# Streaming weight slices in pairs: eight transfers of 768 KB and three buffers in place of fifteen of 384 KB and five

## The chip, the cores and the metric

The kernel runs on one core of a Trainium2 chip. The metric is device time of one execution in microseconds (us). The engines are TensorE (PE, with its weight loads shown as PEld), VectorE (DVE), ScalarE (ACT), GpSimd (POOL) and SyncE (SP, which only issues transfers here).

## The reference

Two attention layers over the same input are mixed by a gate. `A` is recurrent: 64 segments of 32 tokens, and 8 memory rows that each segment hands to the next. All 32 heads of 192 use the same weights in every segment.

```
for s in range(64):                                   # x: [1, 2048, 640], segments of 32
    h = concat([mem, x[:, 32*s:32*s+32]], axis=1)     # 8 + 32 rows of 640
    q, k, v = h @ Wq, h @ Wk, h @ Wv                  # each [640, 32 heads, 192]
    p = softmax(where(mask, q @ k.T * 192**-0.5, -1e9))
    o = (p @ v) @ Wo                                  # [32, 192, 640]
    mem, out_a[s] = o[:, :8], o[:, 8:]
b = sliding_dilated_attention(x, wqkv, wo)            # window 8, dilation 2, 32 heads of 20
g = sigmoid((x * gate_w).sum(-1))
out = g * out_a + (1 - g) * b                         # bf16 in and out
```

## The kernel before

The program has four stages. `part_b` computes layer B and the gate. `prepass` projects the last 8 tokens of every segment ahead of time, into `zpk_dram`. `part_a` is the loop over the 64 segments, the main loop. `part_z` finishes the rows that were left for the end.

The weights Wq, Wk, Wv and Wo are cut into 80 slices of [128, 1536] bf16, 384 KB each: five slices (`kc` 0 to 4) for each of four column blocks `R` of q, k and v, twelve slices `oa` and eight `ob` of Wo. They do not all fit on chip. 65 of them stay resident (tiles `wres_*` and `wlate_*`), and 15 are streamed from DRAM again in every segment through a pool `wstream` of `WBUFS` = 5 buffers, tile name `wst`. `weights_setup` picks the streamed ones: it lays all 80 on an estimated time line of one segment and takes the slice nearest to each of 15 evenly spaced points. They are, in the order of use: q(0,2), k(0,4), q(1,4), q(2,0), k(2,0), q(3,0), k(3,0), v(0,0), v(1,1), v(2,0), v(3,0), oa 0, oa 5, oa 7 and ob 4. The four of Wo are first rewritten into a DRAM scratch `wscr` so that each partition's row is contiguous.

In a segment PE runs, in the order that `part_a` writes down: q and k of the four blocks (`m_qk`, line 540), their transposes (`t_qk`, 554), scores (`s_a` and `s_b`, 577 and 586), v (`m_v`, 623), the softmax sums (`e_norm`), p times v (`pv_half`, 643 and 647), and the output projection (`o_group`, 680). The last part of that order is

```
m_v(2); pv_half(0); e_norm(1); m_v(3)
for i2 in range(6): o_group("oa", i2)
pv_half(1)
for i2 in range(3): o_group("ob", i2)
for i2 in range(6, 12): o_group("oa", i2)
load_z(s + 1)
for i2 in range(3, 12): o_group("ob", i2)
```

so `oa` 0 to 5 come before `pv_half(1)`, and `ob` 0 and 1 come right behind it, before `oa` 6 to 11. The memory rows of the next segment come out of `sel` (line 690) by way of two copies on ACT into `whi` (lines 746 and 754; the profile calls this tile ZQ, of which it is a part). `load_z` (lines 513 and 514) is issued on ACT's queue between these two copies, and brings 96 KB into `KZ` and 96 KB into `ZQ`; the first scores of the next segment read that part of `ZQ`.

The streamed slices are loaded by SP, one transfer for each (`load_slice`, lines 381 and 383). SP issues in program order, and each issue waits until the buffer is free, that is until PE has finished with the slice that came five streamed slices earlier. Each transfer writes 128 rows of 3072 bytes.

Of the kernel before, what the change touches and what calls it, by code (L numbers as in the profile page):

```python
# [10 lines left out]
BF = mybir.dt.bfloat16  # L11
F32 = mybir.dt.float32
I32 = mybir.dt.int32

N_STREAM = 15
N_LATE = 55
N_LATE2 = 22
WBUFS = 5

_DEV = {"mode": "full"}  # L20

# [3 lines left out]
class _K:  # L25
# [313 lines left out]
    def weights_setup(self):  # L339
        nc, tc = self.nc, self.tc  # L340
        keys = self.slice_keys()
        gap = {("q", 0, 3): 200, ("k", 0, 3): 0, ("q", 1, 0): 620, ("k", 1, 0): 270, ("q", 2, 0): 570, ("k", 2, 0): 270,
               ("q", 3, 0): 980, ("k", 3, 0): 270, ("v", 0, 0): 690, ("v", 1, 0): 270, ("v", 2, 0): 710,
               ("v", 3, 0): 1160, ("oa", 6): 1530, ("q", 0, 0): 200}
        at, t = {}, 0
        for k in keys:
            t += gap.get(k, 0)
            at[k] = t
            t += 163
        self.stream_keys = set()  # L350
        for i in range(N_STREAM):
            left = [k for k in keys if k not in self.stream_keys]
            self.stream_keys.add(min(left, key=lambda k: abs(at[k] - (i + 0.5) * t / N_STREAM)))
        rest = [k for k in keys if k not in self.stream_keys]
        first = ["q", "k", "v", "oa", "ob"]
        self.late = sorted(rest, key=lambda k: first.index(k[0]))[-N_LATE:]
        self.wres = self.ctx.enter_context(tc.tile_pool(name="wres", bufs=1))
        self.res_tiles = {}
        self.wscr = {}
        self.early = [k for k in rest if k not in self.late]  # L360
        self.wstream = self.ctx.enter_context(tc.tile_pool(name="wstream", bufs=WBUFS))

    def load_early(self):

        for k in self.early:
            self.res_tiles[k] = self.load_slice(self.wres, k, "wres_" + "_".join(map(str, k)))
        so = sorted(k for k in self.stream_keys if k[0] in ("oa", "ob"))
        scr = self.dram.tile([len(so), 128, 1536], BF, name="wscr")
        for i, k in enumerate(so):
            src, split = self.slice_info(k)  # L370
            self.nc.sync.dma_start(scr[i].rearrange("p (c f) -> p c f", c=split[0]), src)
            self.wscr[k] = scr[i]

    def load_slice(self, pool, key, name, tag=None, t=None):
        src, split = self.slice_info(key)
        kw = {"tag": tag} if tag else {}
        if t is None:
            t = pool.tile([128, 1536], BF, name=name, **kw)
        v = t if split is None else t.rearrange("p (c f) -> p c f", c=split[0])
        if key in self.wscr:  # L380
            self.nc.sync.dma_start(t[:], self.wscr[key])
        else:
            self.nc.sync.dma_start(v[:], src)
        return v

    def load_late(self, part):

        pool = self.ctx.enter_context(self.tc.tile_pool(name=f"wlate{part}", bufs=1, reuse_waits="tile"))
        ks = (self.late[:-N_LATE2], self.late[-N_LATE2:-1], self.late[-1:])[part]
        first = ks[:4] if part == 1 else []  # L390
        place = [k for k in ks if k not in first] + first
        tiles = {k: pool.tile([128, 1536], BF, name="wlate_" + "_".join(map(str, k))) for k in place}
        for k in ks:
            self.res_tiles[k] = self.load_slice(None, k, None, t=tiles[k])

    def get_slice(self, key):
        if key in self.res_tiles:
            return self.res_tiles[key]
        return self.load_slice(self.wstream, key, "wst", "wst")

    def prepass(self):

# [484 lines left out]
```

## Time and profile before

| | |
|---|---|
| median of 3 runs | 1902.32 us (1899.49 to 1911.51) |
| the profiled execution | 1907.39 us, its span 1905.7 us |
| granted TensorE clock, mean over the span | 0.985 |
| `part_b` and the first part of `prepass` | PE begins `ps_pre` (line 425) at 229 us |
| main loop | 411 to 1849 us, 64 segments |
| `part_z` | from 1849 us |
| PE busy in the span | 1729.0 us (91%) |
| DMA, mean of the 16 engines, 800 to 1000 us | busy 0.91, 296 GB/s |
| HBM read over the span | 446.61 MB |

A time in the profile counts from the start of the span. The busy share of PE is that of pipelined matmuls. The DMA share is the mean over 16 engines of the time that their packets took. Queue q1 carries what SP issues, q10 what ACT issues, and q8 the instruction blocks that the engines fetch.

### The profile page before, as it was taken

The page shows a single profiled execution, that of the slowest core. Times are in us where ns is not written, and L with a number is a line of the kernel's source. Part 1 is how long each engine was busy: PE and PEld are TensorE (multiplying, and loading weights), DVE is VectorE, ACT ScalarE, POOL GpSimd, SP SyncE. Part 2 cuts the span into 40 slices and gives each one's busy share as a digit, 9 for nine tenths or more (in the row PEclk, how much of TensorE's full clock was granted, in tenths as well). Part 3 has the DMA queues.
Part 4 walks back from the last instruction along what each step waited for, and adds up shares of the span by engine and source line. Part 5 has one row for each costly group of instructions (what it writes and reads, how often), then busy time and mean ns, then how long its engine had stood idle before and what let it go on. Part 6 is the DMA issues. An engine that isn't in the chain of part 4 may idle for free.

```text
span 1905.7 us, 91340 instructions
## 1 busy us (share of the span) xinstructions
PE 1729.0 (91%) x41120; PEld 1022.0 (54%) x41135; DVE 655.9 (34%) x2047; ACT 743.4 (39%) x1865; POOL 69.5 (4%) x135
## 2 busy tenths in 40 slices
PE   6998999779999999999999899989999999999989
PEld 3554544335555555555555555555555555555557
DVE  4565433223333333333333333333333333333330
ACT  3776522123333343333333333333443333333340
POOL 4010000010000000000000000000000000000000
PEclk9999999989999999999999999999999999999999
DMA  6510395979889899899989888989999898998991
GB/s 176 177 44 16 100 308 137 303 203 291 282 287 297 283 296 292 287 301 292 303 291 296 284 278 290 295 281 287 297 299 293 289 293 284 295 289 282 294 295 31
DMA packets 299434, 486.88 MB, mean 255 GB/s; under 512 B 99236, under 2 KB 168356, under 8 KB 299044
## 3 DMA queue, kind: packets, MB, share of 16 engines
q1 hardware_dynamic: 182680, 420.92, 67.7%
q10 hardware_dynamic: 116364, 60.12, 11.3%
q8 instruction: 322, 5.28, 1.1%
q14 instruction: 68, 0.56, 0.1%
HBM read 446.61 MB, written 35.91 MB: 253 GB/s over the span
## 4 chain that ended last, share of the span: by engine, by line
PE 73%; DMA 9%; ACT 7%; issue 5%; DVE 3%; ACTq 2%; SPq 0%; DVEq 0%
PE ps_qk L540 22%; PE ps_v L623 12%; PE ps_wo L680 10%; PE ps_qkT L554 6%; PE ps_pre L425 5%; DMA ZQ<-zpk_dram 4%; PE ps_S L577 3%; PE ps_bqk L220 3%; PE ps_z L819 3%; PE ps_oT L643 3%; ACT bP L243 2%; DMA zpk_dram<-ZV 2%; DMA wst<-in_A_Wk_dram 2%; ACT KV L545 1%; DVE KV L653 1%
## 5 line engine op out<-in xcount | busy, mean ns | idle before, releaser
L545 ACT CAST KV<-ps_qk 128x384 bf16<-128x384 f32 x512 | 239.4, 480 | 415.0 <-PE ps_qk L540 411.4
L540 PEld LDWEIGHTS <-hT 128*32 128x32 bf16 x10240 | 237.6, 96 | 192.2 <-issue 75.1
L540 PE MATMUL ps_qk<-wlate_k,hT 128*32 128x384 bf16 x4352 | 248.4, 328 | 11.0 <-ACT ZQ L754 6.6
L623 PE MATMUL ps_v<-wlate_v,hT 128*32 128x384 bf16 x4096 | 228.0, 329 | 6.0 <-issue 5.8
L680 PEld LDWEIGHTS <-KV 128*32 128x32 bf16 x6144 | 172.4, 98 | 111.0 <-DVE KV L653 33.6
L540 PE MATMUL ps_qk<-wres_q,hT 128*32 128x384 bf16 x2560 | 164.8, 331 | 28.5 <-ACT KV L545 15.9
L557 DVE COPY ZQ<-ps_qkT 128x384 bf16<-128x384 bf16 x256 | 91.2, 356 | 250.6 <-PE ps_qkT L554 250.2
L680 PE MATMUL ps_wo<-wlate_oa,KV 128*32 128x384 bf16 x2304 | 160.3, 339 | 12.8 <-issue 4.0
L540 PE MATMUL ps_qk<-wst,hT 128*32 128x384 bf16 x1792 | 154.5, 331 | 1.7 <-issue 1.5
L623 PEld LDWEIGHTS <-hT 128*32 128x32 bf16 x5120 | 113.8, 96 | 70.7 <-issue 12.9
L554 PE MATMUL ps_qkT<-ident,KV 128*128 128x128 bf16 x1536 | 141.2, 221 | 3.8 <-DVE ZQ L616 1.7
L653 DVE CAST KV<-ps_oT 128x192 bf16<-128x192 f32 x256 | 79.9, 353 | 186.4 <-ACT KV L653 186.4
L680 PE MATMUL ps_wo<-wlate_ob,KV 128*32 128x256 bf16 x2688 | 134.9, 280 | 10.2 <-issue 10.2
L554 PEld LDWEIGHTS <-KV 128*128 128x128 bf16 x1536 | 87.6, 97 | 95.0 <-issue 93.7
L680 PE MATMUL ps_wo<-wst,KV 128*32 128x384 bf16 (+1 forms) x1152 | 124.1, 319 | 5.4 <-issue 3.5
L653 ACT CAST KV<-ps_oT 128x192 bf16<-128x192 f32 x256 | 69.8, 325 | 123.7 <-PE ps_oT L647 122.2
L540 PE MATMUL ps_qk<-wlate_q,hT 128*32 128x384 bf16 x1536 | 108.3, 330 | 0.0
L577 PE MATMUL ps_S<-ZQ,KV 128*32 128x40 bf16 (+1 forms) x4096 | 99.6, 186 | 8.3 <-DMA ZQ<-zpk_dram 6.8
L577 PEld LDWEIGHTS <-KV 128*32 128x32 bf16 (+1 forms) x4096 | 77.7, 92 | 47.4 <-issue 10.8
L693 DVE CAST hT<-ps_mem 128x24 bf16<-128x24 f32 x126 | 22.6, 179 | 214.6 <-PE ps_mem L690 214.6
L627 ACT CAST KV<-ps_v 128x384 bf16<-128x384 f32 x128 | 61.4, 479 | 84.1 <-DMA a<-bsc_dram 50.7
L623 PE MATMUL ps_v<-wst,hT 128*32 128x384 bf16 x1024 | 89.1, 336 | 1.2 <-issue 1.2
(130 smaller groups left out, 2214.4 us busy)
## 6 DMA issues: line engine op xcount, KB each, us to landing
wst<-in_A_Wq_dram SPq DMA_DIRECT2D x260, 384.0 KB
wst<-in_A_Wv_dram SPq DMA_DIRECT2D x260, 384.0 KB
wst<-wscr SPq DMA_DIRECT2D x256, 384.0 KB
wst<-in_A_Wk_dram SPq DMA_DIRECT2D x195, 384.0 KB
zpk_dram<-ZS ACTq DMA_DIRECT2D x4, 3072.0 KB
ZQ<-zpk_dram ACTq DMA_DIRECT2D x128, 96.0 KB
wlate_k<-in_A_Wk_dram SPq DMA_DIRECT2D x17, 384.0 KB
wlate_v<-in_A_Wv_dram SPq DMA_DIRECT2D x16, 384.0 KB
```

Of the source, the lines that this page charges most:

```text
L220: nc.tensor.matmul(ps[:, 0:nn], lhsT=wqk[n][:, kc, 4 * g:4 * g + 4, :].rearrange("p h d -> p (h d)"), rhs=xT[:, kc, o0:o0 + nn], start=(kc ...
L425: nc.tensor.matmul(ps[:], lhsT=sls[kc][:, c0:c0 + 128], rhs=zT[:, kc, :], start=(kc == 0), stop=(kc == KC - 1))
L540: nc.tensor.matmul(pq[32 * j:32 * j + 32, 0:384], lhsT=hT[:, kc, :], rhs=sl[:, 384 * j:384 * j + 384], start=(kc == 0), stop=(kc == KC - 1 ...
L545: nc.scalar.copy(st, pq[:, 0:384])
L554: nc.tensor.transpose(pT[:, t, :, :, :].rearrange("p j b i -> p (j b i)"), st[:, 128 * t:128 * t + 128], self.ident[:])
L557: nc.vector.tensor_copy(q_blocks(R)[:, 1:5, :, :].rearrange("p b c i -> p c b i"), pT.rearrange("p t j b i -> p (t j) b i"))
L577: nc.tensor.matmul(pSs[h][32 * j:32 * j + 32, par, 40 * r:40 * r + 40], lhsT=KT[k0:k1, 12 * r + c, :], rhs=q_blocks(R)[k0:k1, :, c, :], st ...
L623: nc.tensor.matmul(pv[32 * j:32 * j + 32, 0:384], lhsT=hT[:, kc, :], rhs=sl[:, 384 * j:384 * j + 384], start=(kc == 0), stop=(kc == KC - 1 ...
L627: nc.scalar.copy(V[R], pv[:, 0:384])
L643: nc.tensor.matmul(out[:, r, t, :], lhsT=V[2 * h + r][ks, f0:f1], rhs=E[ks, par, 40 * r:40 * r + 40], start=(r == 0 and t == 0), stop=Fals ...
L653: cp(oTxs[2 * h + j // 2][:, 6 * (j % 2):6 * (j % 2) + 6, :], pos[j // 2][:, j % 2, 0:240].rearrange("p (c q) -> p c q", q=40)[:, :, 8:40])
L680: nc.tensor.matmul(pso[part][32 * jj:32 * jj + 32, 0:n], lhsT=oTxs[2 * (R // 2) + j // 2][:, 6 * (j % 2) + 3 * (R % 2) + t, :], rhs=o_weig ...
```

## The change

Streamed slices are chosen, loaded and freed in neighbouring pairs. `N_STREAM` goes from 15 to 16 and `WBUFS` from 5 to 3, with buffers of twice the size. 64 slices stay resident instead of 65. The pairs, in order of use, are k(0,0-1), k(1,0-1), k(2,2-3), k(3,0-1), v(1,0-1), v(2,2-3), oa 4-5 and ob 0-1. One transfer writes 256 runs of 3072 bytes (q, k, v) or 128 runs of 6144 bytes (from `wscr`). A pair's transfer is issued where its first slice is asked for, and its buffer is free when PE has finished with the second.

```diff
-N_STREAM = 15
+N_STREAM = 16
-WBUFS = 5
+WBUFS = 3
...
-        for i in range(N_STREAM):
-            left = [k for k in keys if k not in self.stream_keys]
-            self.stream_keys.add(min(left, key=lambda k: abs(at[k] - (i + 0.5) * t / N_STREAM)))
+        pairs = [(k, k[:-1] + (k[-1] + 1,)) for k in keys
+                 if k[-1] % 2 == 0 and not (k[0] in "qkv" and k[-1] == self.KC - 1)]
+        self.pairs, self.held, self.stream_keys = {}, {}, set()
+        for i in range(N_STREAM // 2):
+            left = [p for p in pairs if p[0] not in self.stream_keys]
+            p = min(left, key=lambda p: abs((at[p[0]] + at[p[1]]) / 2 - (i + 0.5) * t / (N_STREAM // 2)))
+            self.stream_keys.update(p)
+            self.pairs.update({k: p for k in p})
...
-        scr = self.dram.tile([len(so), 128, 1536], BF, name="wscr")
+        scr = self.dram.tile([128, len(so), 1536], BF, name="wscr")
...
+    def load_pair(self, first):
+
+        src, split = self.slice_info(first)
+        t = self.wstream.tile([128, 2, 1536], BF, name="wst", tag="wst")
+        if first in self.wscr:
+            self.nc.sync.dma_start(t[:], self.wscr[first])
+            return [t[:, i, :].rearrange("p (c f) -> p c f", c=split[0]) for i in range(2)]
+        W = {"q": self.Wq, "k": self.Wk, "v": self.Wv}[first[0]].rearrange("(c p) f -> p c f", p=128)
+        self.nc.sync.dma_start(t[:], W[:, first[2]:first[2] + 2, first[1] * 1536:(first[1] + 1) * 1536])
+        return [t[:, i, :] for i in range(2)]
...
     def get_slice(self, key):
         if key in self.res_tiles:
             return self.res_tiles[key]
-        return self.load_slice(self.wstream, key, "wst", "wst")
+        p = self.pairs[key]
+        if key == p[0]:
+            self.held.update(zip(p, self.load_pair(key)))
+        return self.held[key]
```

## The prediction

> **What bounds the kernel now.** I read the page first, then the main loop alone (411 to 1849 us): PE's waits, the DMA queues, the chain of waits, and the timeline of one segment.
>
> ```profile
> span 1905.7 us, 91340 instructions
> PE 1729.0 (91%) x41120; PEld 1022.0 (54%) x41135; DVE 655.9 (34%) x2047; ACT 743.4 (39%) x1865; POOL 69.5 (4%) x135
> PE 73%; DMA 9%; ACT 7%; issue 5%; DVE 3%; ACTq 2%; SPq 0%; DVEq 0%
> ```
>
> PE is the bound: 91% busy, 73% of the chain. So the change can gain only from PE's idle 9%, and costs whatever it adds there. PE's own waits in the main loop (time, number, longest):
>
> ```profile
> PE ps_oT L643 <- issue: 20.6, 19, 2.2
> PE ps_wo L680 <- issue: 17.6, 23, 1.3
> ...
> PE ps_oT L647 <- issue: 12.2, 10, 2.4
> ...
> PE ps_S L577 <- DMA ZQ<-zpk_dram: 6.8, 10, 1.6
> PE ps_qk L540 <- ACT ZQ L754: 6.6, 17, 1.3
> ```
>
> No line says that PE waits for `wst`: five buffers are enough. The largest waits are "issue", 67.3 us in all (20.6 + 17.6 + 12.2, and 8.2 + 7.0 + 1.2 + 0.5 in rows left out). In the trace the stalls above 0.4 us fall 256 PE instructions apart or a multiple of it, and end some 1.4 us after a packet of queue q8 has ended. They are waits for instruction blocks, which share the DMA engines with the weights. The queues in the main loop:
>
> ```profile
> q1 hardware_dynamic: 144132, 380.51, 80.7%
> q10 hardware_dynamic: 63687, 32.59, 8.0%
> q8 instruction: 283, 4.64, 1.3%
> ```
>
> The weights (q1) hold the DMA engines 80.7% of the time, everything together 90.1%. One 384 KB slice costs 0.807 x 1438 us / 968 slices (380.51 MB / 0.393 MB) = 1.20 us of all 16 engines. How long a load takes from issue to use is in the chain, where it passes through one:
>
> ```profile
> 586.98 4.42 DMA wst<-in_A_Wk_dram
> ...
> 787.27 3.67 DMA wst<-in_A_Wk_dram
> ...
> 1210.14 4.94 DMA wst<-in_A_Wk_dram
> 1232.43 4.08 DMA wst<-in_A_Wk_dram
> ...
> 1388.94 4.09 DMA wst<-in_A_Wk_dram
> ```
>
> 3.67 to 4.94 us, the middle 4.09, against a lead of five streamed slices, about 7 us of a 22.4 us segment (1438 / 64).
>
> **The change, part by part.** The matmuls are the same in number and order, so PE's work stays. `part_b`, `prepass` and `part_z` get 0: the loads for them run in `part_b`, where the engines have room (44 and 16 GB/s in two slices of the page). The first main-loop load on SP waits for the release of k(3)'s buffer at the end of the q and k prepass before as after, so the late loads queued behind it start as before; if that slipped, it would cost the slip once, a few us.
>
> *Fewer issues, -3 us.* SP has 8 transfers a segment to issue instead of 15, each 0.33 us in the timeline, and it spends the time between waiting for PE; nothing waits for the issuing itself. One thing may gain: ACT's two issues of `load_z` stand ahead of the copy of line 754, and took up to 1.25 us on the chain where SP was issuing too, against 0.39 elsewhere. After the change the SP issues around the segment's edge are the release of ob (3.7 us before it) and that of k(0) (1.3 us behind it), clear of both. The bounds are 0 and all of the two waits in question, 6.6 (line 754) and 6.8 (line 577 for ZQ), so -13. ZQ still meets a busy q1, so I take half of the first.
>
> *A sixteenth slice, +12 us.* q1 goes to 80.7 x 16/15 = 86.1%, all queues to 95.4%. PE does not wait for this share as such, but for the blocks of q8. Reading the 283 q8 packets of the main loop one by one against the DMA share around each, the time from the previous block's edge to the packet's end grows by about 2 us per unit of share, so 0.11 us for 5.4 points. Shifting every block by 0.1 us adds 11 us of stalls in this trace (75 stall already, the rest have some slack), so 0.11 us adds 12. Low bound (a gain is excluded, since nothing fetches sooner under more load): stalls grow only with the share, 67.3 x 0.054/0.901 = +4. High bound: they grow as the room shrinks, from 9.9 to 4.6 points; half of that doubling, since the fully loaded 230 to 250 us (share 1.01) show no wait longer than the main loop's, +38.
>
> The Trainium skill, "Runtime: NRT & Kernel Launch", section "Instruction fetch mechanics", states the 16 KiB blocks of 256 instructions that these stalls show, but says that fetching is hidden behind issue. The trace differs, with 67.3 us. By the page this part would be 0 and the total 12 us lower. Another page speaks against the change: "DMA: Bandwidth & Descriptors", "Queues, rings and completion order", has an engine drain a whole packet of 9 to 17 descriptors from one queue before it turns to the next. By that, an engine's 16 descriptors of a pair would hold a block or a ZQ row up for twice as long as 8, an estimate of half a slice, 0.6 us a block and some +75 us. In the trace at 923 us single 768-byte packets of q10 alternate with single 3072-byte packets of q1, so I leave it out.
>
> *Three double buffers, +16 us.* A pair is one transfer with one semaphore: its first slice waits until both have landed. The shortest lead is from the release of the pair v(1,0-1) to the first use of ob 0, three pairs on. v(1,1) is streamed before too, so one segment shows both ends (here the second is the resident ob 0):
>
> ```profile
> 935.84 0.34 PE L623 MATMUL ps_v<-wst,hT 128*32 128x384 bf16 x4
> ...
> 941.50 0.51 PE L680 MATMUL ps_wo<-wlate_ob,KV 128*32 128x256 bf16 x12
> ```
>
> From 936.18 to 941.50 are 5.32 us. Over all segments the trace gives 4.99 at the short end and 5.36 in the middle. A pair needs the middle row's 4.09 plus one more slice, 1.20: 5.29 us. It lands when it is wanted. With loads between 3.67 and 4.94 it is late in about half of the segments; I take 0.25 us on average, x64 = 16. The bounds: 3.67 + 0.98 (a slice at the 402 GB/s that the windows show from 240 to 250 us) = 4.65, never late, 0, and no gain, since no wait for `wst` is there to be removed; 4.94 + 1.20 = 6.14, late by 0.82 each time, 52. Being late has no cover: SP's next issue and all of PE stand behind it. The next tightest lead, k(2) to v(2), read the same way, is 6.2 us, and has 0.9 to spare; the others have 7.5 and more.
>
> *Sum:* -3 + 12 + 16 = +25 us. On the profiled execution, 1907.4 (span 1905.7 and 1.7 around it), that is 1932.4. That execution stands 5.1 above the median of the runs, 1902.3, so I forecast 1927 for the median. The runs lie 0.6% apart, so about 1% (19 us) can be told from no change.
>
> **The rivals.**
>
> *The stream becomes the bound (slower, 1968).* Where an engine imbalance or HBM holds the share near the 0.90 to 0.93 that the main loop never leaves for long, 16 slices take 22.4 x 0.954/0.93 = 23.0 us a segment, +0.6 us x 64 = 38, and up to 22.4 x 0.954/0.901 = 23.7, +84. The middle, with the ob stall inside it, is +61: 1963, and with the fetch stalls partly on top 1968. For it: PE, the fetches and the stream meet in the same engines. Against: 230 to 250 us moved 378 GB/s, and 16 slices with the rest need only 305 (6.8 MB in 22.4 us).
>
> *Hidden anyway (no change, 1903).* The pair arrives within the lead, since a stall of PE for an instruction block lengthens the lead too, and a wait for ob lets the next block arrive. Then only +4 and -3 are left. For it: the lead's upper half goes beyond 5.4 us. Against: the pair's price has no room at the middle.
>
> *Gain at the segment's edge (not slower, 1885).* The one mechanism: between the releases of ob and k(0) SP issues nothing for some 5 us, so `load_z` is issued and lands without rivals. The chain gives ZQ's load 4% and ACTq 2%. It removes 6.8 + 6.6 of PE's waits and, with q1 quieter there, part of the stalls of lines 540 and 577. Its price is -13 to -24, 1878 to 1889. It decides if ZQ lands in under 5 us where it took 5.1 to 7.1, and ob is not late. Against: ob's own release starts a 2.4 us transfer that still runs when ZQ's begins.
>
> **How the numbers follow.** Forecast 0.50 (1910 to 1945, of which 0.35 is over 1% slower and 0.15 within 1%); stream as the bound 0.18, all slower; hidden anyway 0.14 (0.12 within 1%, 0.02 faster); gain 0.18, faster. Together slower 0.53, same 0.27, faster 0.20. The range runs from 1885, the gain's middle, to 1980, near the +84 of the bound stream: about one in ten is left out on either side.
>
> **What would show it.** Right: q1 moves 25 MB more (64 x 0.39), its share of the main loop is near 86%, "issue" waits on PE are near 80 us, and line 680 with the 128x256 shape waits for `wst<-wscr` in about half of the segments, some 16 us. SP waits for PE, not the reverse, everywhere else. Wrong: no wait at ob, or waits for `wst` at k and v as well (then the stream is the bound), or `issue` waits that fall although the share rises; then the price I put on the sixteenth slice is not one of share.

## The result and the profile after

| | before | after |
|---|---|---|
| median (lowest to highest), 4 runs each | 1900.9 us (1891.2 to 1911.5) | 2024.2 us (2010.8 to 2030.0) |
| ratio, 95% interval | | 1.0665 (1.0624 to 1.0706) |
| the profiled execution | 1907.4 us | 2027.6 us |
| granted TensorE clock, mean over the span | 0.985 | 0.962 |
| main loop | 411 to 1849 us | 412 to 1968 us |
| a segment | 22.5 us | 24.3 us |

The changed kernel is 6.7% slower; the forecast was 1927 us, and its range ended at 1980. Nearly the whole difference, 117 of the 120 us between the two profiled executions, is in the main loop: 1439 us became 1556, while the time ahead of it (411 and 412 us) and behind it (56 and 58 us) stayed. The page of the changed kernel, its span, busy times and shares of the chain:

```profile
span 2025.9 us, 90370 instructions
PE 1766.2 (87%) x41120; PEld 1039.2 (51%) x41135; DVE 655.6 (32%) x2047; ACT 746.1 (37%) x1865; POOL 69.6 (3%) x135
PE 67%; DMA 14%; issue 8%; ACT 6%; DVE 3%; ACTq 2%; SPq 0%; DVEq 0%
```

PE has the same 41120 matmul records and is busy 37 us longer (1729.0 to 1766.2), 35 of them in the main loop (1322 to 1357). It also stands still longer: from the trace, the time of the main loop in which neither PE nor PEld works grew from 114 to 197 us, +83. The two make 118, which is the difference. What PE waits for in the main loop (411 to 1970 us; line numbers are 15 higher than before):

```profile
PE ps_oT L658 <- issue: 44.2, 29, 2.7
PE ps_wo L695 <- issue: 38.7, 30, 2.5
PE ps_oT L662 <- issue: 22.7, 14, 3.6
...
PE ps_wo L695 <- DMA wst<-wscr: 8.7, 14, 1.2
PE ps_S L592 <- DMA ZQ<-zpk_dram: 6.6, 11, 1.5
...
PE ps_v L638 <- DMA wst<-in_A_Wv_dram: 4.3, 9, 1.2
...
PE ps_qk L555 <- ACT ZQ L769: 1.7, 5, 0.5
```

Waits for `wst` are new, but small: 13.0 us. The growth is in "issue", 146.4 us over all rows against 67.3. By the trace these are again stalls at the edges of 256-instruction blocks: 118 of more than 0.2 us, 148 us in all, against 75 and 72 us before. The time from the previous block's edge to the start of the next block's packet went from 2.00 to 2.49 us in the middle, and from 2.50 to 3.32 us at the upper quarter. Yet the queues are no fuller (queue: packets, MB, share of the 16 engines):

```profile
q1 hardware_dynamic: 129856, 406.13, 80.6%
q10 hardware_dynamic: 65131, 32.68, 7.3%
q8 instruction: 283, 4.64, 1.2%
```

q1 moved 25.6 MB more, as it had to, in a loop that was 8% longer, so its share is 80.6% where it was 80.7%. All queues together went from 0.901 to 0.892.

The longer busy time comes with a slower clock. These are windows of the changed kernel around one stall (stretch, its length, busy PE, PEld, DVE, ACT and POOL with counts, granted clock, DMA share, GB/s), and PE's own timeline in the same place:

```profile
668.00:672.00 4.00, 3.55 (x128) 2.13 (x128) 1.76 (x8) 1.75 (x6) 0.00 (x0) 1.00 0.91 284
672.60:675.29 2.69, 1.04 (x40) 0.51 (x39) 0.23 (x1) 0.54 (x2) 0.00 (x0) 1.00 1.00 334
675.29:678.70 3.41, 3.36 (x48) 2.00 (x45) 0.55 (x3) 0.72 (x2) 0.00 (x0) 0.50 0.84 251
```

```profile
670.07 0.82 PE L695 MATMUL ps_wo<-wlate_oa,KV 128*32 128x384 bf16 x16
...
674.19 0.17 PE L662 MATMUL ps_oT<-ZQ 32*128 32x32 bf16 x1 [2.64 <-issue]
...
675.08 2.49 PE L695 MATMUL ps_wo<-wlate_oa,KV 128*32 128x384 bf16 x24
```

PE waits 2.64 us for a block while the DMA engines are full (share 1.00). Then the clock is 0.50 for 3.41 us. Ahead of the stall 16 matmuls of 128x384 took 0.82 us, 0.05 each; behind it 24 of the same shape take 2.49 us, 0.10 each, and PE is shown as busy throughout. Such stretches begin on a fixed grid of 3.41 us, mostly behind a gap of 1.5 to 3.6 us; not every such gap is followed by one (PE waits 2.69 us up to 523.73, and the clock stays at 1.00). The main loop had 9 of them, 31 us, before, and has 30, 119 us, after. At half clock work takes twice as long, so the 89 us more account for up to 44 us of busy time, an estimate, against the 35 measured.

### The profile page after: what moved, and what is told of

Same layout as the page of the kernel before. It is cut to its first block, busy times and chain, and to the rows that moved or that the text cites. A ratio compares the mean times of both kernels' runs of the same rounds, so it can differ in the third digit from the quotient of the medians.

```text
span 2025.9 us, 90370 instructions
## 1 busy us (share of the span) xinstructions
PE 1766.2 (87%) x41120; PEld 1039.2 (51%) x41135; DVE 655.6 (32%) x2047; ACT 746.1 (37%) x1865; POOL 69.6 (3%) x135
## 4 chain that ended last, share of the span: by engine, by line
PE 67%; DMA 14%; issue 8%; ACT 6%; DVE 3%; ACTq 2%; SPq 0%; DVEq 0%
PE ps_qk L555 20%; PE ps_wo L695 11%; PE ps_v L638 9%; PE ps_qkT L569 5%; PE ps_pre L440 5%; DMA ZQ<-zpk_dram 5%; DMA wst<-wscr 4%; PE ps_z L834 3%; PE ps_S L592 3%; PE ps_bqk L220 3%; PE ps_oT L658 2%; ACT bP L243 2%; DMA wst<-in_A_Wv_dram 2%; DMA zpk_dram<-ZV 2%; ACT KV L560 1%
## 5 line engine op out<-in xcount | busy, mean ns | idle before, releaser
L695 PEld LDWEIGHTS <-KV 128*32 128x32 bf16 x6144 | 183.5, 103 | 139.3 <-issue 54.0
L638 PE MATMUL ps_v<-wlate_v,hT 128*32 128x384 bf16 x4096 | 234.0, 333 | 13.8 <-issue 13.5
L555 PE MATMUL ps_qk<-wlate_k,hT 128*32 128x384 bf16 x3072 | 196.2, 330 | 4.9 <-issue 4.7
L695 PE MATMUL ps_wo<-wlate_oa,KV 128*32 128x384 bf16 x2560 | 172.0, 364 | 21.2 <-issue 13.8
L555 PE MATMUL ps_qk<-wlate_q,hT 128*32 128x384 bf16 x2816 | 174.5, 332 | 0.7 <-issue 0.5
L555 PE MATMUL ps_qk<-wres_q,hT 128*32 128x384 bf16 x2304 | 147.3, 340 | 30.6 <-ACT KV L560 15.2
L638 PEld LDWEIGHTS <-hT 128*32 128x32 bf16 x5120 | 114.7, 96 | 87.4 <-issue 31.7
L555 PE MATMUL ps_qk<-wst,hT 128*32 128x384 bf16 x2048 | 143.8, 333 | 8.9 <-issue 6.5
L695 PE MATMUL ps_wo<-wlate_ob,KV 128*32 128x256 bf16 x2304 | 107.4, 297 | 11.1 <-issue 11.1
L658 PE MATMUL ps_oT<-ZQ,KV 32*128 32x40 bf16 (+1 forms) x4096 | 72.4, 187 | 44.2 <-issue 44.2
L592 PEld LDWEIGHTS <-KV 128*32 128x32 bf16 (+1 forms) x4096 | 78.8, 92 | 54.1 <-issue 17.6
L708 DVE CAST hT<-ps_mem 128x24 bf16<-128x24 f32 x126 | 22.5, 179 | 253.7 <-PE ps_mem L705 251.5
L695 PE MATMUL ps_wo<-wst,KV 128*32 128x256 bf16 (+1 forms) x1280 | 78.2, 318 | 22.9 <-issue 13.8
```

What stands on the lines that cost most here:

```text
L555: nc.tensor.matmul(pq[32 * j:32 * j + 32, 0:384], lhsT=hT[:, kc, :], rhs=sl[:, 384 * j:384 * j + 384], start=(kc == 0), stop=(kc == KC - 1 ...
L592: nc.tensor.matmul(pSs[h][32 * j:32 * j + 32, par, 40 * r:40 * r + 40], lhsT=KT[k0:k1, 12 * r + c, :], rhs=q_blocks(R)[k0:k1, :, c, :], st ...
L638: nc.tensor.matmul(pv[32 * j:32 * j + 32, 0:384], lhsT=hT[:, kc, :], rhs=sl[:, 384 * j:384 * j + 384], start=(kc == 0), stop=(kc == KC - 1 ...
L658: nc.tensor.matmul(out[:, r, t, :], lhsT=V[2 * h + r][ks, f0:f1], rhs=E[ks, par, 40 * r:40 * r + 40], start=(r == 0 and t == 0), stop=Fals ...
L695: nc.tensor.matmul(pso[part][32 * jj:32 * jj + 32, 0:n], lhsT=oTxs[2 * (R // 2) + j // 2][:, 6 * (j % 2) + 3 * (R % 2) + t, :], rhs=o_weig ...
```

## The experiments

Each line of results gives the median of its 4 runs (10 for the one with 14 slices), the ratio to the kernel before with its 95% interval, and from its profile the main loop, PE's "issue" waits in it, PE's waits for `wst`, and the half-clock stretches. The kernel before ran again beside each group of them, with medians of 1897.7 to 1904.2 us, and the ratios are to these. In the profile before, the main loop and the waits are 1439 us, 67.3, 0 and 9 (31 us); after, 1556, 146.4, 13.0 and 30 (119 us).

### The change taken apart

*Two transfers for a pair.* The changed kernel with each pair loaded as two transfers of 384 KB:

```diff
-            self.nc.sync.dma_start(t[:], self.wscr[first])
+            for i in range(2):
+                self.nc.sync.dma_start(t[:, i, :], self.wscr[first][:, i, :])
...
-        self.nc.sync.dma_start(t[:], W[:, first[2]:first[2] + 2, first[1] * 1536:(first[1] + 1) * 1536])
+        for i in range(2):
+            self.nc.sync.dma_start(t[:, i, :], W[:, first[2] + i, first[1] * 1536:(first[1] + 1) * 1536])
```

> The paired kernel with each pair loaded by two transfers of 384 KB instead of one of 768 KB; slices, buffers and release points unchanged. Theory A (the size of one transfer: 16 descriptors per engine in one go hold the instruction blocks up, and the first slice waits for both): about 1930 us, PE's issue waits in the main loop back from 146 to some 80 us. Theory B (which 16 slices, and freeing them in pairs, keep the queue fuller at the wrong times): within 15 us of the paired kernel's 2024, issue waits near 140 us, only the waits for wst fall. Theory C (the 6144-byte rows of the scratch): falls as well, since the rows are 3072 again, to about 1960.

1972.99 us, 1.0381 (1.0311 to 1.0450); main loop 1508; issue 114.7, `wst` 8.5, 23 stretches (92 us).

*The same 16 slices one by one.* The kernel before with the changed kernel's choice of slices (its loop over `pairs` in `weights_setup`), single loads and six buffers:

```diff
-N_STREAM = 15
+N_STREAM = 16
...
-WBUFS = 5
+WBUFS = 6
...
-        self.stream_keys = set()
-        for i in range(N_STREAM):
...
+        for i in range(N_STREAM // 2):
...
+            self.stream_keys.update(p)
```

> The same 16 slices as the paired kernel, but loaded and freed one by one through six buffers of 384 KB, the same space. Theory A: about 1915 us, issue waits 70 to 80 us. Theory B, if the choice of slices (neighbours, used back to back) is what hurts: about 2000 us; if the freeing in pairs is, about 1920. A pure price of the sixteenth slice (rival D, the stream as the bound): 1960 or more.

1981.89 us, 1.0421 (1.0347 to 1.0495); main loop 1509; issue 106.6, `wst` 5.8, 28 stretches (106 us).

*Sixteen spaced slices.* The kernel before with one more slice, still chosen at even spacing, five buffers:

```diff
-N_STREAM = 15
+N_STREAM = 16
```

> The kernel before with 16 evenly spaced single slices and its five buffers. My prediction priced the sixteenth slice at +12 us (4 to 38): 1905 to 1940, middle 1913. Rival D (the stream is the bound): 1960 or more. Theories A, B and C: at most 1920.

1939.83 us, 1.0205 (1.0139 to 1.0271); main loop 1465; issue 84.9, `wst` 0.6, 9 stretches (38 us).

These three make a ladder. The sixteenth slice costs 2% by itself. The changed kernel's choice of slices costs another 2% (1982 against 1940) with single loads and the same amount of data; it had six buffers and the spaced slices five, but spaced slices with six (the bursts below) take 1945. Freeing in pairs with three buffers costs nothing that can be told (1973 against 1982). One transfer in place of two costs 51 us (2024 against 1973; the intervals lie apart).

*Rows of 3072 bytes from the scratch.* The changed kernel with `wscr` laid out slice by slice, so that its pairs too are written in runs of 3072 bytes, still in one transfer:

```diff
-        scr = self.dram.tile([128, len(so), 1536], BF, name="wscr")
+        scr = self.dram.tile([len(so), 128, 1536], BF, name="wscr")
...
-                self.wscr[k] = scr[:, i:i + 2, :]
+                self.wscr[k] = scr[i:i + 2].rearrange("k p f -> p k f")
```

> The paired kernel with the scratch laid out by slice again, so that a pair of Wo comes as 256 rows of 3072 bytes instead of 128 of 6144, still one transfer. Theory C (large descriptors block the engines): about 1970 us, with fewer issue waits at lines 658, 662 and 695. Theories A, B and D: no change, 2010 to 2035.

2010.41 us, 1.0560 (1.0474 to 1.0646); main loop 1558; issue 140.9, `wst` 12.0, 36 stretches (143 us). The long rows are not the cause: the interval overlaps that of the changed kernel, and the main loop and the block stalls are the same.

### Size, number and bursts of single loads

*Half slices by partitions.* The kernel before with each slice loaded as two transfers of 64 partitions:

```diff
+        halves = [(0, 128)] if tag is None else [(0, 64), (64, 128)]
+        for p0, p1 in halves:
...
+                self.nc.sync.dma_start(v[p0:p1], src[p0:p1])
```

> The kernel before (15 slices, five buffers) with each slice loaded by two transfers of 64 partitions, 4 rows of 3072 bytes on each engine instead of 8. Bytes, slices and buffers unchanged. Theory A (what one transfer queues on an engine in one go delays the instruction blocks): less than before, 1880 to 1895, issue waits under 60 us. Theory E (only the bytes and the moment they are asked for count): 1900 to 1910, and issue waits of 65 to 75 us. Twice as many issues on SP (30 x 0.33 us of a 22 us segment) leave it room in both.

2399.45 us, 1.2628 (1.2563 to 1.2693); main loop 1932; issue 3.7, `wst` 411.2. As a test of the size this failed. A 3072-byte packet of q1 took 198 ns in the middle where it took 121, so the DMA engines moved 216 GB/s over the main loop at a share of 0.89, and PE waited for weights. It shows what a stream that is the bound looks like: waits at every streamed line, hardly any for blocks.

*Fewer slices.* The kernel before with 14 slices and four buffers, and (with 13 and 3 in the same places) with 13 slices and three:

```diff
-N_STREAM = 15
+N_STREAM = 14
...
-WBUFS = 5
+WBUFS = 4
```

> The kernel before with 14 streamed slices and four buffers, the same space on chip. With +36 us measured for the sixteenth slice, theory D (each streamed slice has a price, since PE's instruction blocks share the engines) says about 1875 us, issue waits 50 to 60 us. If the price of a slice starts only above 15 (the engines are full there), 1895 to 1905. If four buffers are too few, waits for wst appear.

1903.18 us, 1.0025 (0.9985 to 1.0065); main loop 1429; issue 55.2, `wst` 6.0, 7 stretches (31 us). No difference: less for blocks, a little for weights.

> The kernel before with 13 streamed slices and three buffers. Theory D: 1850 us if three slices of lead, about 5.2 us, cover a load of 4 to 5 us; if not, waits for wst in the main loop and 1880 or more.

1926.67 us, 1.0150 (1.0094 to 1.0205); main loop 1441; issue 21.4, `wst` 72.2, one stretch. With three single buffers PE waits for weights; two rows of its waits in the main loop:

```profile
PE ps_qk L540 <- DMA wst<-in_A_Wq_dram: 27.9, 42, 1.7
PE ps_wo L680 <- DMA wst<-wscr: 24.3, 39, 2.0
```

*Bursts of two.* Sixteen spaced slices, six single buffers, and two loads issued back to back whenever the first of two is asked for:

```diff
+            for k in (self.use_order[i + 1], key):
+                self.held[k] = self.load_slice(self.wstream, k, "wst", "wst")
```

> 16 evenly spaced single slices as in the run with 1939.8 us, with six buffers, but in the main loop always two slices are asked for together, the later-used one first, so that SP issues two transfers back to back, eight times a segment. If it is the bursts that made the neighbouring slices dearer (1982 against 1940), this gives 1970 or more with issue waits above 100 us. If it is which slices are streamed, and so where in the segment the loads fall, it stays at 1935 to 1950.

1944.71 us, 1.0228 (1.0178 to 1.0279); main loop 1478; issue 90.1, `wst` 0.3, 17 stretches (61 us). Within the interval of the sixteen spaced slices: issuing in twos is not what makes the neighbours dear.

### The place of ob, the size of a transfer, and no stream at all

*ob 4-5 in place of ob 0-1.* The changed kernel and its two-transfer form, with the pair that I had feared would be late moved back in the segment, by taking the candidates ahead of it off the list in `weights_setup`:

```diff
-                 if k[-1] % 2 == 0 and not (k[0] in "qkv" and k[-1] == self.KC - 1)]
+                 if k[-1] % 2 == 0 and not (k[0] in "qkv" and k[-1] == self.KC - 1) and k not in [("ob", 0), ("ob", 2)] + [("oa", i) for i in (6, 8, 10)]]
```

> The paired kernel, one transfer a pair, with the pair ob 4-5 streamed instead of ob 0-1: it is used and freed some 3 us later in the segment, so the loads of v, oa and ob no longer crowd into the stretch of p times v and the output projection, where PE runs through an instruction block fastest. Theory F (it is the place of the loads in the segment that made neighbouring slices dearer): 1975 to 1990 us, issue waits of lines 658, 662 and 695 down by a third, no waits for wst at ob. Theory A alone (the size of a transfer): 2005 to 2030.

2015.49 us, 1.0583 (1.0518 to 1.0647); main loop 1547; issue 143.2, `wst` 5.8, 29 stretches (113 us).

> The same slices as in the run before it, with two transfers of 384 KB a pair. Theory F: 1935 to 1950, no dearer than 16 evenly spaced slices (1940). If it is not the place: about 1973, as with ob 0-1.

1972.52 us, 1.0362 (1.0309 to 1.0415); main loop 1505; issue 121.7, `wst` 1.6, 24 stretches (92 us). All waits for `wst` at `ob` are gone, and what is gained is no more than they were: 9 us in the first, with overlapping intervals, and nothing in the second. The late pair was real and small.

*Four transfers for a pair* in the changed kernel, 192 KB each (half the columns of a slice, runs of 1536 bytes):

```diff
+            for i in range(2):
+                for h in (slice(0, 768), slice(768, 1536)):
+                    self.nc.sync.dma_start(t[:, i, h], self.wscr[first][:, i, h])
```

> The paired kernel with four transfers of 192 KB a pair (128 partitions, rows of 1536 bytes). One transfer gave 2010 to 2024, two gave 1973. Theory A (what one transfer queues in one go delays the instruction blocks): lower again, 1940 to 1955. Theory G (two transfers gained only because the first slice arrives by itself, and because SP waits less for a slot): 1965 to 1980. With 40 transfers a segment SP may have to wait for earlier transfers to land before it issues; then waits for wst appear and it is above 2000.

2044.56 us, 1.0744 (1.0691 to 1.0796); main loop 1577; issue 28.3, `wst` 24.2, 29 stretches (106 us). Most of the block stalls vanish, and the time does not. A row of PE's waits from 420 to 1840 us, and one of ACT's:

```profile
PE ps_qk L560 <- ACT ZQ L774: 87.9, 55, 3.5
```

```profile
ACT ZQ L774 <- DMA wst<-in_A_Wk_dram: 128.7, 54, 4.3
```

PE waits for the copy that makes the memory rows, and that copy waits on ACT behind an issue of `load_z`, which in turn is shown waiting for a weight transfer to land. This wait is the program's own. In the trace all transfers, those of SP and of ACT, tell of their landing through the same eight semaphores, and here each of the 2494 issues of the main loop waits on its own one, that is for the transfer that last used it, whichever queue had issued that. So no more than eight transfers are ever under way in the main loop, in this run and in all the others.

*No stream.* The kernel before without the reload in the main loop. This leaves out the streamed weights: one buffer, loaded once, stands for all 15 slices.

```diff
-        return self.load_slice(self.wstream, key, "wst", "wst")
+        if not hasattr(self, "still"):
+            self.still = self.load_slice(self.wstream, ("q", 0, 2), "wst", "wst")
```

> The kernel before with no weight streaming: one buffer, filled once, stands for all 15 streamed slices (so their products use wrong weights, and nothing is reloaded). It prices the stream as a whole. If PE's instruction waits come from sharing the engines with it, they fall from 67 to under 15 us and with them the dips of the clock: 1810 to 1835 us. If the blocks are late by themselves, 1870 or more.

1809.41 us, 0.9511 (0.9470 to 0.9552); main loop 1343. PE's "issue" waits in its main loop, both rows, and a window that answers to the main loop's middle:

```profile
PE ps_v L626 <- issue: 0.5, 2, 0.3
PE ps_oT L650 <- issue: 0.4, 1, 0.4
```

```profile
800.00:1000.00 200.00, 193.63 (x5402) 117.57 (x5399) 70.00 (x258) 81.87 (x229) 5.09 (x10) 1.00 0.11 28
```

This is the key to the case. The same matmuls and blocks, at a DMA share of 0.11, stall for 0.9 us in all. The stream never makes PE wait for a weight in the kernel before, and yet it costs 94 us there (1903.4, the kernel before beside this run, less 1809.4). Of the 96 us in the profiled main loop, 66 are "issue" waits and 23 are busy time of PE (1322 to 1299). The half-clock stretches, 31 us before and 7 here, are worth some 12 of the 23, an estimate; what the rest is was not split.

### Rows, columns and place

*Rows of 1536 bytes.* The kernel before, one transfer for each slice, the two halves of every row written to places 32 bytes apart so that the runs are 1536 bytes (the buffer is 32 elements wider):

```diff
+        halves = t.rearrange("p (h x) -> p h x", h=2)[:, :, 0:768]
+        self.nc.sync.dma_start(halves, flat.rearrange("p (h x) -> p h x", h=2))
```

> The kernel before (15 slices, five buffers, one transfer a slice), but in the main loop each partition's slice is written as two runs of 768 elements with a gap of 32 bytes, so that a descriptor moves 1536 bytes instead of 3072. Theory H (the size of a row decides how long an instruction block queues): issue waits fall from 67 to 30 us, time 1850 to 1870. Theory A (the bytes that one transfer queues): no change, 1895 to 1910, or slower by the smaller rows' overhead.

1920.85 us, 1.0115 (1.0085 to 1.0145); main loop 1453; issue 80.9, `wst` 0.2, 12 stretches (44 us). Shorter runs do not shorten the block stalls.

*Two transfers for a slice.* The kernel before, half the columns in each:

```diff
+        for h in (slice(0, 768), slice(768, 1536)):
+            self.nc.sync.dma_start(t[:, h], flat[:, h])
```

> The kernel before with two transfers of 192 KB a slice (columns 0 to 767 and 768 to 1535), so rows of 1536 bytes and 30 transfers a segment. If the issue waits fall here and not with one transfer of the same rows: theory A, the size of a transfer. If they fall in both: theory H. I expect 35 us of issue waits and, as with four transfers a pair, new waits of ACT's copies behind its own transfers, 1890 to 1930.

1942.52 us, 1.0225 (1.0193 to 1.0257); main loop 1482; issue 36.3, `wst` 1.7, 10 stretches (38 us). The runs are as in the kernel just told, the transfers half as large, and the block stalls less than half. The gain is lost again on ACT's queue, as with four transfers (here too each of the 2368 issues waits on its own semaphore); PE's waits from 420 to 1840 us:

```profile
PE ps_qk L542 <- ACT ZQ L756: 48.4, 49, 2.3
```

*The same with `load_z` earlier*, to take it out of the way of that copy:

```diff
+                if s + 1 < nseg:
+                    load_z(s + 1)
                 pv_half(1)
...
-                    load_z(s + 1)
```

> Two transfers of 192 KB a slice, and the loads for the next segment's memory scores issued on ACT before the second p times v instead of between the two copies of the output projection. If ACT's queue is what ate the gain of small transfers: 1850 to 1880, no waits for ACT's copy at line 540. If the waits only move, 1900 or more.

2199.11 us, 1.1572 (1.1529 to 1.1615); main loop 1720; issue 16.6, `wst` 0.2, 64 stretches (393 us). It failed by a new wait: a copy on POOL into the shared ZQ space now holds up p times v, and there are as many half-clock stretches as segments. From 420 to 1840 us:

```profile
PE ps_oT L645 <- POOL ZQ L517: 216.1, 53, 6.0
```

*Other pairs*, chosen to keep the stream out of the places with most stalls, two transfers each:

```diff
+        chosen = [("k", 0, 0), ("k", 1, 0), ("k", 2, 0), ("q", 3, 0), ("k", 3, 2), ("v", 3, 2), ("oa", 4), ("ob", 4)]
```

> Pairs in two transfers as in the run with 1973 us, but the pairs are k(0,0-1), k(1,0-1), k(2,0-1), q(3,0-1), k(3,2-3), v(3,2-3), oa 4-5, ob 4-5: none is freed between v(0) and the second half of v, where before the pairs v(1) and v(2) are. Theory F (the place of the loads: those released at v run while PE goes through p times v): 1935 to 1955, issue waits at lines 660 and 664 halved. If not the place: 1965 to 1985.

2004.26 us, 1.0566 (1.0506 to 1.0626); main loop 1539; issue 100.3, `wst` 23.9, 26 stretches (96 us). Worse than the two-transfer kernel by 31 us. Cutting each segment of the trace into elevenths, q1 was busy 0.24 of one of them and up to 0.96 of others (0.63 to 0.92 in the changed kernel). Between k(3,2-3) and v(3,2-3) nothing comes free for some 5.8 us, and the other pairs crowd.

### Even spacing

The last two runs follow from that miss. The trace without a stream gives the time of each slice's first use in an undisturbed segment of 21.0 us. From one streamed pair to the next (the last figure leads into the next segment) it is

| pairs | us between first uses |
|---|---|
| changed kernel | 3.3, 2.8, 2.2, 3.0, 1.5, 2.9, 1.2, 4.2 |
| with ob 4-5 | 3.3, 2.8, 2.2, 3.0, 1.5, 2.9, 3.3, 2.0 |
| the other pairs above | 3.3, 2.5, 1.2, 1.7, 5.8, 1.2, 3.3, 2.0 |
| even | 2.5, 2.5, 2.6, 2.8, 2.7, 2.5, 2.4, 3.0 |

against 2.4 us that the engines need for a pair. (The expectation gives the changed kernel's as 0.9 to 4.1, a rougher reading.) The even set, with two transfers and with one:

```diff
+        chosen = [("q", 0, 0), ("q", 1, 0), ("q", 2, 0), ("q", 3, 0), ("v", 0, 0), ("v", 2, 0), ("oa", 0), ("oa", 6)]
```

> Eight pairs of neighbours as two 384 KB transfers each, three pair buffers, as in the two-transfer kernel, but other pairs: q(0,0-1), q(1,0-1), q(2,0-1), q(3,0-1), v(0,0-1), v(2,0-1), oa 0-1, oa 6-7. In the run without a stream the first uses of these lie 2.4 to 2.8 us apart all through the segment; those of the changed kernel's pairs lie 0.9 to 4.1 us apart. Theory E (uneven spacing): pairs that come free close together queue up behind each other, and the rest of the segment leaves q1 with nothing to do; the blocks meet the packed part. It expects the cost of the neighbours to go: main loop 1465 to 1480 us as for 16 spaced slices, time 1940 to 1950, issue waits 85 to 95 us, half-clock stretches 10 to 17. Rival N (neighbours cost by themselves, wherever they lie): 1965 to 1980 as in the two-transfer kernel, issue waits near 115 us. A place in the segment that matters for itself would show as a time away from both.

1938.30 us, 1.0225 (1.0202 to 1.0248); main loop 1458; issue 82.3, `wst` 0.5, 12 stretches (44 us).

> The same evenly spaced pairs, each loaded by one transfer of 768 KB; row lengths and buffers as in the changed kernel. Against the run with two transfers this prices the transfer's size without the packing of the layout. Theory S (a larger transfer holds blocks up longer): 35 to 50 us above the even kernel with two transfers, so about 1980 to 2000 if Theory E holds there, issue waits 115 to 125 us, and still some 25 to 40 us below the changed kernel. Rival (the size cost only because the uneven pairs queued behind each other): within 10 us of the even kernel with two transfers. Rival N: 2010 to 2025, as the changed kernel.

1966.22 us, 1.0381 (1.0346 to 1.0417); main loop 1472; issue 100.5, `wst` 0, 16 stretches (58 us). The same window of the two (two transfers first):

```profile
800.00:1000.00 200.00, 181.02 (x4969) 109.22 (x4968) 64.48 (x238) 76.75 (x215) 4.56 (x9) 0.99 0.92 305
```

```profile
800.00:1000.00 200.00, 180.51 (x4949) 108.03 (x4945) 64.73 (x237) 75.36 (x212) 4.56 (x9) 0.99 0.93 301
```

and that of the changed kernel:

```profile
800.00:1000.00 200.00, 172.30 (x4568) 102.80 (x4564) 59.01 (x216) 69.91 (x193) 4.07 (x8) 0.95 0.87 280
```

With an even set, sixteen neighbours cost what sixteen spaced slices cost. So it is not the neighbouring that is dear but which pairs were taken, 35 us with two transfers (1973 to 1938) and 58 with one (2024 to 1966); each less the kernel before beside it, 28 and 55. The single transfer costs 28 us here and 51 in the changed kernel. (The profiles show less of the 28: the profiled execution with one transfer was the fastest of its four, and of the 18 us between the two, 5 lie ahead of the main loop.) One transfer in place of two thus has a price on even pairs too, and a higher one where the pairs crowd. The even kernels do more work at a higher share, 0.92 and 0.93, than the changed one at 0.87: the share does not order the block stalls.

What orders them in the traces is how much the stream had asked for ahead: the bytes that SP had issued on q1 less those that its packets had moved, as a mean over the main loop.

| kernel (loads) | asked for, not yet moved | "issue" |
|---|---|---|
| no stream | 9 KB | 0.9 us |
| two transfers for a slice (192 KB) | 447 KB | 36.3 us |
| four transfers for a pair (192 KB) | 449 KB | 28.3 us |
| 13 slices, three buffers (384 KB) | 479 KB | 21.4 us |
| 14 slices, four buffers (384 KB) | 544 KB | 55.2 us |
| before (384 KB) | 574 KB | 67.3 us |
| even pairs, two transfers (384 KB) | 633 KB | 82.3 us |
| sixteen spaced slices (384 KB) | 640 KB | 84.9 us |
| changed, two transfers (384 KB) | 658 KB | 114.7 us |
| even pairs, one transfer (768 KB) | 743 KB | 100.5 us |
| changed kernel (768 KB) | 760 KB | 146.4 us |

Over all twenty kernels the two columns have a rank correlation of 0.96, and loads of the same 384 KB range from 21.4 to 114.7 us. In the changed kernel alone, block by block, the time from a block's edge to the next block's packet goes with the bytes outstanding at that edge (correlation 0.71, some 1.0 us for 384 KB).

What stays open: the spacing does not order all the runs (moving ob evened it out and gained nothing with two transfers), so the place of the pairs may matter beside it; the even set also differs in streaming q and not k. The even pairs stall less than the changed kernel's at nearly the same amount outstanding (100.5 against 146.4 us at 743 and 760 KB). And whether a transfer's size holds blocks up by itself was not separated from how much is asked for ahead of them: no run changed the one without the other, since with 192 KB transfers the eight semaphores hold the stream back. The table speaks for the amount; it does not show it as the cause. No version that reloads the weights beats the kernel before.

## Why the prediction was wrong

The profiled main loop, by the runs: 1439 us before; 1458 with sixteen slices in even pairs, two transfers each, three buffers (+19); 1508 with the changed kernel's pairs (+50); 1556 with one transfer for each (+48). By the medians, each less the kernel before beside it, the steps are 41, 28 and 54; the even pairs also lose 11 us ahead of the main loop, and the profiled execution before was one of the slower. The prediction's sum was +25, of the size of the first step at most, and had no term for the other two.

*Fewer issues, -3: right in size.* The wait of line 754 (now 769) went from 6.6 to 1.7 us; that for ZQ stayed, 6.8 to 6.6. That SP's issues were the reason was not tested. (ACT's issues on the chain before went up to 1.54 us, and not 1.25 as I had read.)

*A sixteenth slice, +12: right in kind, too small.* The spaced sixteen cost +26 in the profiled main loop and +36 by medians, near the upper bound of 38; "issue" rose by 17.6 us, and the clock had little part in it (9 stretches, as before). The forecast of 86% for q1 was wrong too, since I divided by an unchanged segment: it is 82.9% there, and 80.6% in the changed kernel. (For all queues 90.1 and 5.4 make 95.5, not 95.4.)

*Three double buffers, +16: near in size, by luck.* PE waited 13.0 us for `wst`, but only 8.7 at `ob`, in 14 waits and not in half of the 64 segments; the other 4.3 came at v, where I had seen none. I priced a pair's load at the middle row of 4.09 us plus a slice, 5.29, against a lead of 5.36. In the trace of the changed kernel ob's pair takes 5.6 us in the middle, and the lead from the release of v(1,0-1) to ob 0 has grown to 6.5 (5.5 before, read the same way), since the stalls of PE lengthen it too, as the rival "hidden anyway" had said: load and lead were both longer than I had them, and the two errors offset each other. In the chain of the changed kernel (start, length, transfer) loads take 5.22 to 7.55:

```profile
494.72 7.55 DMA wst<-wscr
...
586.38 6.45 DMA wst<-in_A_Wv_dram
...
1494.53 5.22 DMA wst<-wscr
```

The 1.20 us of a slice were an average over a stream that had room; a pair that comes free soon after another queues behind it. The loads of k(0,0-1) and k(2,2-3) are issued when v(2) and ob come free, 1.5 and 1.2 us behind the pair before by the table above, and take 6.3 and 6.4 us in the middle, the other six 4.9 to 5.6. I had read only the leads (a pair's release to its next use), and from them the rest of the pairs looked safe. I had not read the spacing of the releases against the 2.4 us of a load. SP's own rows look like the same crowding and are not: in the changed kernel's main loop it is shown waiting for earlier transfers to land 174 times, 144 us in all (10 times and 5.5 us before), mostly in these rows,

```profile
SPq L395 <- DMA wst<-wscr: 65.2, 87, 1.9
SPq L395 <- DMA wst<-in_A_Wk_dram: 41.8, 39, 2.5
```

but by the trace SP goes on waiting for PE to free the buffer behind all but one of these waits, so they held no load up.

*The step that failed: pricing the blocks by share.* From the slope of block time against share I took 0.11 us a block. The share did not rise (0.901 to 0.892) and the blocks became later, by 0.5 us in the middle and 0.8 at the upper quarter, and stalled PE for 146.4 us in place of 67.3. What the slope could not hold is how the same share is made up: how large each transfer is and how much is asked for ahead. With the changed kernel's pairs, blocks stalled PE for 146.4 us with transfers of 768 KB, 114.7 with 384 KB and 28.3 with 192 KB; in the kernel before for 67.3 with 384 KB and 36.3 with 192 KB. But the amount outstanding fell with the size each time (760, 658 and 449 KB; 574 and 447), so the size alone is not shown to be the cause. Shorter rows did not help (140.9 with short rows from the scratch, 80.9 with rows of 1536 bytes).

The prediction had weighed the rule of the Trainium skill, "DMA: Bandwidth & Descriptors", section "Queues, rings and completion order", that an engine drains a whole packet of descriptors from one queue before it turns to the next, and left it out, because at one moment packets of two queues were seen to alternate. The trace does not say which of the 16 engines moved a packet, so that reading says nothing of the order on one engine and was no ground to drop the rule. The runs agree with its direction, 48 us in the main loop for the step from two transfers to one against the estimate of +75, but with an even set the same step is 14 us, and no run here shows the order of an engine's packets.

*A term that was missing: the clock.* The prediction let a stall of PE cost its own length. In the runs a stall of some 2 us can be followed by 3.41 us at half clock; PE's busy time in the main loop rose by 35 us with 21 more such stretches, three tenths of the loss. That blocks came only 0.5 us later in the middle hides this: the clock falls behind the long stalls, and "issue" waits of 1.5 us and more went from 9 to 42.

The Trainium skill, "TensorE: Matmul & The Clock Gate", "Part 1: The HAM clock gate", gives the window as 3413 ns, free-running, with half rate after an idle window; the 3.41 us grid of the trace agrees. Its price for time at half clock, half of that time, makes 44 us of the 89 added, an estimate, against the measured 35. It asks for about 3.4 us of idleness, where gaps of 1.5 to 2.6 us were often enough here.

*The rivals.* "The stream becomes the bound" came nearest in time (1968, up to +84) and is still wrong in its mechanism: it wanted a share near 0.93 and PE waiting for weights, and the changed kernel has 0.892 and 13.0 us. The run with half slices by partitions shows what it would have looked like. "Hidden anyway" and "gain at the segment's edge" fell with the result, though the longer lead that the first had named did come. One of the signs I had named, waits for `wst` at v, did come (4.3 us) without the cause that I had tied to it.

## What to carry to other kernels

When PE's waits are for instruction blocks, a weight stream is priced by what it does to those blocks, and the share of the DMA engines does not say it: ask how much the stream asks for ahead, how large each transfer is, and whether the buffers come free about as evenly as the engines can refill them. Fewer and larger transfers for the same data gained little on the issuing side here, since SP was mostly waiting anyway, and cost 28 to 51 us; smaller ones ran into the program's eight landing semaphores, which made the other queue's issues wait. A wait that a profile names is worth nothing until it is clear that nothing else was waited for behind it. A run without the stream, one buffer standing for all, tells in one go what the stream costs where no row names it.

## What the hardware showed that was not expected

- Stalls of PE of some 2 us can halve its clock for 3.41 us, or for two or three times that, on a grid of 3.41 us; the profile then shows PE as busy, so the loss hides in busy time (1729.0 to 1766.2 us). What counts is how long PE stands still within one interval of the grid: over the main loops of all twenty profiles, an interval at full clock with 2.1 us or more was followed by half clock in 164 of 164 cases, one with 1.5 to 2.1 us in 266 of 394, and one with less than 1.2 us in none of 7463.
- Instruction blocks at a DMA share of 0.11 never stalled PE for more than 0.4 us; at one share of 0.89 they stalled it for 3.7 us (half slices by partitions), 28.3 us (four transfers) or 146.4 us (changed kernel), depending on how it was made up.
- Transfers to 64 partitions were slow: 198 ns for a 3072-byte packet where those to 128 partitions took 121, and 216 GB/s in the main loop at a share of 0.89 where there were 291 at 0.90.
- The wait for an instruction block grew with the bytes that the stream had outstanding: from a block's edge to the next block's packet it took 1.56 us in the middle with 449 KB outstanding (four transfers), 2.00 with 574 KB (before) and 2.49 with 760 KB (changed kernel).
